# A two-layer expert network behind Nyström attention: the second activation from ACT's table of mish

## The chip, the cores and the metric

The kernel runs on one core of one Trainium2 chip. The metric is the device time of one execution in microseconds (us). The time before is 887.63 us, the median of three runs (885.74 to 888.40). Engines are named as the profile names them: PE is TensorE's matmul, PEld its weight load, DVE is VectorE, ACT is ScalarE, POOL is GpSimd, SP is the queue that issues the DMAs.

## The reference

Attention in Nyström form over 4 batches, 8 heads, 576 positions and a head size of 64 gives 2304 rows of 512. Two feed-forward layers follow, each with a width of 2048:

```python
h = x @ w_in                      # layer 1
x = (h / (1 + exp(-h))) @ w_out   # silu
h = x @ w_in2                     # layer 2
sp = where(h > 20, h, log1p(exp(min(h, 20))))
out = (h * tanh(sp)) @ w_out2     # mish
```

The change touches the second layer alone.

## The kernel before

**Split numbers.** A product is made of three matmuls: each operand is held as a rounded part (fp32r) and a low part, the difference to the exact value, and high times high, high times low and low times high are summed in one bank of PSUM. So an activation ends in two steps: a rounding copy `gh` and a subtraction `gl = z - gh`.

**Second layer (from L1015).** It goes over 6 blocks (`i`) of 384 tokens, and in each over 16 slices (`j`) of 128 of the inner width: 96 steps `t`, here hh(t) and o(t). hh(t) is 12 matmuls of 384 columns (`h_matmuls`, four parts of the 512 inputs by three terms, recorded at L609), into bank 5 + t mod 3. Then `mish_steps` makes gh(t) and gl(t) from that bank. o(t) is 9 matmuls of 512 columns (`out_matmuls`, L1106: three groups of 128 tokens by three terms), which add to three output banks over the 16 slices of a block. With the last slice `out_block` copies the three banks out (L1069 on ACT; in the last block also L1071, L1074, L1075) and SP stores them (L1077).

**Activation before.** With e = exp(min(h, 20)) and n = e(e + 2), mish is h·n/(n + 2). The kernel makes it in ten instructions: L1033 DVE (min, from PSUM), L1034 ACT (Exp), L1038 and L1039 DVE (n, and n·h, again from PSUM), L1040 and L1041 ACT (Ln of n + 2, then Exp of its negative: r = 1/(n + 2)), L1043, L1044 and L1046 DVE (a Newton step on r, and the product, with its sign turned), L1047 ACT (gh) and L1050 POOL (gl; DVE in the last two steps). The outputs have the sign turned back when they are copied out.

**Order of the work.** PE, ACT and DVE run this layer in the order in which the program names the instructions; POOL and SP are ordered by the compiler's scheduler. At step t PE gets hh(t) and then o(t-2). `mish_steps` is a generator whose parts are woven: in step t the first part of t, then the third part of t-1, the second part of t, and the fourth of t-1. At the end the order is written by hand in `due`: no o at t = 93, o(91) at 94, o(92) and o(93) at 95, then o(94), then o(95).

**What else runs in it.** In steps 0 and 1 PE finishes layer 1 (`emit_y`), whose four banks are copied out at L687 (ACT) and L689 (DVE) and stored by SP (L691). In the first six steps the last six slices of the second layer's `w_out` are loaded (L935), rounded on ACT (L603) and given a low part on POOL (L604). From j = 4 of each block the next block's inputs are loaded (L916), and from j = 6 on rounded on ACT (L920) and given a low part on POOL (L921).

The lines that the change and the prediction name: L125 to L128 (the constant `two`), L1018 (the load of ACT's table), L1027 to L1051 (`mish_steps`), L1069 to L1075 (copies out), L1091 to L1093 and L1124 to L1146 (the loop's order).

Of the kernel before, what the change touches and what calls it, by code (L numbers as in the profile page):

```python
# [8 lines left out]
F32 = mybir.dt.float32  # L9
# [4 lines left out]
AF = mybir.ActivationFunctionType  # L14
ALU = mybir.AluOpType
# [4 lines left out]
P = 128  # L20
# [5 lines left out]
NB2 = 384  # L26
LAG = 2
LAG2 = 2
# [62 lines left out]
def nystrom_moe_kernel(ctx, tc, q, k, v, w1i, w1o, w2i, w2o, out):  # L91
# [4 lines left out]
    NF = FF // P  # L96
# [4 lines left out]
    act, dve, pool, pe, sp = nc.scalar, nc.vector, nc.gpsimd, nc.tensor, nc.sync  # L101
    act.preload_act_table_set("exp_and_others")

    cp = ctx.enter_context(tc.tile_pool(name="cp", bufs=1))
# [17 lines left out]
    mask4 = cp.tile([P, 4], F32, name="mask4")  # L122
    sel2 = cp.tile([P, 2], F32, name="sel2")
    blk = cp.tile([P, P], F32, name="blk")
    two = cp.tile([P, 1], F32, name="two")  # L125
    for t in (mask2, mask4, sel2, blk):
        pool.memset(t, 0.0)
    pool.memset(two, 2.0)  # L128
    for h2 in range(2):
        pool.memset(mask2[64 * h2 : 64 * h2 + 64, h2 : h2 + 1], 1.0 / (G * 8.0))  # L130
    for h in range(4):
# [9 lines left out]
    def bank(i, name):  # L141
        return ps.tile([P, 512], F32, tag=f"b{i}", name=name)
# [502 lines left out]
    def h_matmuls(hb, w, x, n):  # L645
        (wh, wl), (xh, xl) = w, x
        for dt in range(ND):
            mm3(hb[:, :n], [(wh[:, dt], xh[:, dt]), (wh[:, dt], xl[:, dt]), (wl[:, dt], xh[:, dt])], dt == 0, dt == ND - 1)

    def after(later, earlier, reason="activation tables"):  # L650
        tc.add_manual_dep(
            later.ins,
            earlier.ins.name,
            mybir.DependencyInfo(mybir.DependencyClass.NoSync, mybir.DependencyReason.DATA),
            reason=reason,
        )
# [222 lines left out]
    nblk = NT // HB  # L879
    steps = [(i, j) for i in range(2, nblk) for j in range(NF)]  # L880
    ybank = {}
    gt = {}
# [26 lines left out]
    def y_load(i, pl):  # L909
        yh = pl.tile([P, ND, NB2], F32R, tag=f"yh{i % 2}", bufs=1, name=f"yh{i}")  # L910
        yl = pl.tile([P, ND, NB2], F32R, tag=f"yl{i % 2}", bufs=1, name=f"yl{i}")
        raws = []

        def load(t):
            raw = late["pool"].tile([P, 512], F32, tag=f"raw{t % 2}", bufs=2, name=f"yr{i}_{t}")
            sp.dma_start(raw[:, :NB2], ysc[t * P : (t + 1) * P, i * NB2 : (i + 1) * NB2])  # L916
            raws.append(raw)

        def part(t):
            act.copy(yh[:, t], raws[t][:, :NB2])  # L920
            pool.tensor_tensor(yl[:, t], raws[t][:, :NB2], yh[:, t].bitcast(F32), op=ALU.subtract)  # L921

        return (yh, yl), load, part
# [36 lines left out]
    def gtiles(t, n):  # L960
        gt_ = wp.tile([P, 2, n], F32R, tag=f"gt{t % 3}", name=f"g{t}_{n}")
        return gt_[:, 0], gt_[:, 1]

    def emit_y(t):
        i, j = steps1[t]
        if j == 0:
            ybank[i] = [bank(m, f"y{i}_{m}") for m in range(ND)]
        y_matmuls(ybank[i], wout[j], *gt.pop(("a", t)), j == 0, j == NF - 1)
        if j == NF - 1:
            y_out(ybank[i], i)  # L970
# [3 lines left out]
    for t in range(len(steps)):  # L974
        i, j = steps[t]
# [6 lines left out]
        if i == nblk - 1 and j == 0:  # L982
# [3 lines left out]
            ycur, yload, ypart = y_load(0, late["pool"])  # L986
            wgen = [second_weights(0), second_weights(1)]
        hb = bank((4, 6)[t % 2], f"h{t}")
# [26 lines left out]
    lft.close()  # L1015


    tables = act.preload_act_table_set("natural_log_exp_and_others")  # L1018
    for x in tanhs[-4:]:
        after(tables, x)  # L1020
    m2 = ctx.enter_context(tc.tile_pool(name="m2", bufs=2))
    late["tail"], late["lo"] = m2, pool
    nblk = NT // NB2
    NCH = NB2 // P
    steps = [(i, j) for i in range(nblk) for j in range(NF)]

    def mish_steps(t, h):  # L1027

        e = m2.tile([P, NB2], F32, tag="e", bufs=3, name=f"e{t}")
        n = m2.tile([P, NB2], F32, tag="n", bufs=2, name=f"n{t}")  # L1030
        r = m2.tile([P, NB2], F32, tag="r", bufs=2, name=f"r{t}")
        z = m2.tile([P, NB2], F32, tag="z", bufs=2, name=f"z{t}")
        dve.tensor_scalar(e, h, 20.0, None, op0=ALU.min)  # L1033
        ins = act.activation(e, e, AF.Exp)  # L1034
        if t == 0:
            after(ins, tables)
        yield
        dve.scalar_tensor_tensor(n, e, 2.0, e, op0=ALU.add, op1=ALU.mult)  # L1038
        dve.tensor_tensor(e, n, h, op=ALU.mult)  # L1039
        act.activation(r, n, AF.Ln, bias=two)  # L1040
        act.activation(r, r, AF.Exp, scale=-1.0)  # L1041
        yield
        dve.scalar_tensor_tensor(z, n, 2.0, r, op0=ALU.add, op1=ALU.mult)  # L1043
        dve.scalar_tensor_tensor(z, z, -2.0, r, op0=ALU.add, op1=ALU.mult)  # L1044
        gh, gl = gt[t] = gtiles(t, NB2)
        dve.tensor_tensor(z, z, e, op=ALU.mult)  # L1046
        act.copy(gh, z)  # L1047
        yield
        eng = pool if t < nblk * NF - 2 else dve
        eng.tensor_tensor(gl, z, gh.bitcast(F32), op=ALU.subtract)  # L1050
        yield  # L1051

    def out_rows(o):

        if o // S in dve_tr:
            return [(0, P, out[o : o + P, :])]
        parts, n = [], 0
        while n < P:
            b, c, r = (o + n) // S, (o + n) % S // PT, (o + n) % PT
            k = min(P - n, PT - r)  # L1060
            parts.append((n, n + k, out[b * S : (b + 1) * S, :].rearrange("(p c) n -> c p n", c=NC)[c, r : r + k]))
            n += k
        return parts

    def out_block(i):
        for c in range(NCH):
            ot = m2.tile([P, DM], F32, tag="ot", bufs=3, name=f"ot{i}_{c}")
            if i < nblk - 1 or c == 0:
                act.mul(ot, obank[i][c], -1.0)  # L1069
            elif c == 1:  # L1070
                dve.tensor_scalar(ot, obank[i][c], -1.0, None, op0=ALU.mult)  # L1071
            else:
                h = DM // 2
                act.mul(ot[:, :h], obank[i][c][:, :h], -1.0)  # L1074
                dve.tensor_scalar(ot[:, h:], obank[i][c][:, h:], -1.0, None, op0=ALU.mult)  # L1075
            for r0, r1, rows in out_rows(i * NB2 + c * P):
                sp.dma_start(rows, ot[r0:r1])  # L1077

# [9 lines left out]
                part(dt)  # L1088
                yield

    mish, ys, obank = {}, {0: ycur}, {}  # L1091
    n = len(steps)
    due = {3: (), 2: (n - 5,), 1: (n - 4, n - 3), 0: (n - 2,), -1: (n - 1,)}  # L1093

    def out_matmuls(t):
        i, j = steps[t]
        gh, gl = gt.pop(t)
        wh, wl = wout2[j]
        if j == 0:
            obank[i] = [bank((NCH * i + c + 4) % 5, f"o{i}_{c}") for c in range(NCH)]  # L1100
        order = [(c, k) for k in range(3) for c in range(NCH)]
        if t == len(steps) - 1:
            order = [(0, 0), (0, 1), (1, 0), (1, 1), (0, 2), (1, 2), (2, 0), (2, 1), (2, 2)]
        for c, k in order:
            a, w = ((gh, wh), (gh, wl), (gl, wh))[k]
            pe.matmul(  # L1106
                obank[i][c],
                a[:, c * P : (c + 1) * P],
                w,
                start=j == 0 and k == 0,  # L1110
                stop=j == NF - 1 and k == 2,
            )
        if j == NF - 1:
            out_block(i)

    with tc.manual_schedule(engines={act.engine, dve.engine, pe.engine}):
        for t in range(len(steps) + LAG2):
            if t < len(steps):
                i, j = steps[t]
                while j not in win2:  # L1120
                    next(wgen[0])
                hb = bank(5 + t % 3, f"hh{t}")
                h_matmuls(hb, win2[j], ys[i], NB2)
                mish[t] = mish_steps(t, hb[:, :NB2])  # L1124
                next(mish[t])
                for x in (mish.get(t - 1), mish[t]) if t < len(steps) - 1 else (mish[t], mish[t - 1]):
                    if x:
                        next(x)
                if t:
                    next(mish[t - 1])  # L1130
                if i == 0:
                    next(wgen[0], None)
                    next(wgen[1], None)
                if t < LAG:
                    emit_y(len(steps1) - LAG + t)
                if j == 4:
                    ygen = next_y(i + 1)
                if j >= 4:
                    next(ygen, None)
            elif t == len(steps):  # L1140
                next(mish[t - 1])
                next(mish[t - 1])

            for ty in due.get(len(steps) - t, (t - LAG2,)):
                if ty >= 0:
                    out_matmuls(ty)  # L1146


_INS = ["q", "k", "v", "moe_w_in", "moe_w_out", "moe2_w_in", "moe2_w_out"]
# [25 lines left out]
```

## Time and profile before

| | before |
|---|---|
| median of three runs | 887.63 us (885.74 to 888.40) |
| span of the profiled execution | 886.1 us |
| PE busy | 851.9 us (96%) |
| DVE busy | 648.5 us (73%) |
| ACT busy | 475.5 us (54%) |
| POOL busy | 290.3 us (33%) |

The span runs from the first instruction to the last in one profiled execution. Nothing is listed of that execution beside its span, which lies 1.5 us under the median of the runs and within their spread. A busy time counts how long an engine had at least one instruction in work; matmuls overlap each other, so a row's mean duration of a matmul is longer than the distance from one matmul's start to the next. The chain of waits follows the work that ended last back through the program; where PE stands in it for long stretches without a break, PE sets the pace there.

### The profile page before, as it was taken

What the parts mean: (1) busy time and instruction counts of PE and PEld (TensorE: products, weight loads), DVE (VectorE), ACT (ScalarE), POOL (GpSimd) and SP (SyncE); (2) the same over time, 40 slices, a digit from 0 to 9 for tenths busy, and PEclk for the clock granted to TensorE, in tenths of its full rate; (3) what the DMA queues carried; (4) which work ended last, traced back from release to release, by engine and by line L of the source; (5) the groups of instructions that cost most, each with busy time, mean ns of one, the idle gap of its engine ahead of it and who ended that gap; (6) DMA issues with size and microseconds to landing.
All of it is one profiled execution on the core that took longest, in us unless ns stands there. A gap on an engine that the chain in (4) does not pass through costs nothing.

```text
span 886.1 us, 15069 instructions
## 1 busy us (share of the span) xinstructions
PE 851.9 (96%) x5424; PEld 740.1 (84%) x5424; DVE 648.5 (73%) x1289; ACT 475.5 (54%) x1045; POOL 290.3 (33%) x331
## 2 busy tenths in 40 slices
PE   6889999999999898999999999999999999999997
PEld 5656777769998797889899889999998998998996
DVE  3878878778586868743565987787787787787776
ACT  4657555355445555654565555555555455555543
POOL 1311323034433446534333432232242242242221
PEclk8779999999999999999999999999999999999999
DMA  8735475344363466812551111000110110000000
GB/s 229 200 98 147 155 211 155 70 125 97 97 141 116 115 212 221 274 52 73 171 169 56 51 27 26 20 28 18 27 27 12 34 28 5 32 1 1 36 1 36
DMA packets 95355, 79.63 MB, mean 90 GB/s; under 512 B 52528, under 2 KB 80688, under 8 KB 95280
## 3 DMA queue, kind: packets, MB, share of 16 engines
q1 hardware_dynamic: 95280, 78.67, 30.8%
q8 instruction: 42, 0.69, 0.3%
q14 instruction: 33, 0.27, 0.1%
HBM read 60.82 MB, written 17.83 MB: 89 GB/s over the span
## 4 chain that ended last, share of the span: by engine, by line
PE 74%; DVE 8%; issue 5%; POOL 4%; ACT 4%; DMA 3%; SPq 1%; POOLq 0%; DVEq 0%; ACTq 0%
PE hh L609 21%; PE o L1106 21%; PE y L609 11%; PE h L609 5%; PE ya L835 5%; PE ha L635 4%; POOL g L667 2%; PE u L524 2%; DMA q<-in_q_dram 2%; PE nw L421 2%; DVE z L1044 1%; PE cv L372 1%; DVE rawt L596 1%; POOL rawt L591 1%; SPq L201 1%
## 5 line engine op out<-in xcount | busy, mean ns | idle before, releaser
L1050 POOL TENSOR_TENSOR g<-z,g 128x384 fp32r<-128x384 f32 x94 | 95.9, 1020 | 258.8 <-ACT g L1047 256.5
L1106 PE MATMUL o<-wh,g 128*128 128x512 f32 x576 | 166.3, 396 | 2.7 <-ACT g L1047 1.5
L609 PE MATMUL y<-g,wh 128*128 128x288 f32 x768 | 163.0, 302 | 5.6 <-POOL g L667 1.8
L609 PEld LDWEIGHTS y<-g,wh 128*128 128x128 f32 x768 | 124.5, 190 | 15.2 <-ACT th L664 4.1
L667 POOL TENSOR_TENSOR g<-g,g 128x288 fp32r<-128x288 f32 x96 | 81.2, 846 | 169.6 <-ACT g L666 140.3
L609 PE MATMUL hh<-yh,wi2h 128*128 128x384 f32 x384 | 130.4, 339 | 0.0
L609 PE MATMUL hh<-yh,wi2l 128*128 128x384 f32 x384 | 129.6, 338 | 0.0
L609 PE MATMUL hh<-yl,wi2h 128*128 128x384 f32 x384 | 129.5, 337 | 0.0
L1106 PEld LDWEIGHTS o<-wh,g 128*128 128x128 f32 x576 | 106.4, 188 | 23.5 <-ACT g L1047 3.7
L1047 ACT CAST g<-z 128x384 fp32r<-128x384 f32 x96 | 49.3, 514 | 132.2 <-DVE z L1046 132.2
L609 PE MATMUL y<-g,wl 128*128 128x288 f32 x384 | 114.0, 297 | 0.0
L1033 DVE TENSOR_SCALAR e<-hh 128x384 f32<-128x384 f32 x96 | 53.5, 557 | 69.3 <-PE hh L609 69.1
L609 PE MATMUL h<-ath,uw 128*128 128x288 f32 x384 | 95.2, 302 | 1.1 <-DVE uw L544 1.1
L1106 PE MATMUL o<-wl,g 128*128 128x512 f32 x288 | 82.2, 393 | 0.0
L1034 ACT ACTIVATE e<-e 128x384 f32<-128x384 f32 x96 | 50.3, 524 | 55.2 <-DVE e L1033 54.7
L665 DVE SCALAR_TENSOR_TENSOR g<-th,h 128x288 f32<-128x288 f32 x96 | 42.9, 447 | 50.4 <-ACT th L664 48.1
L609 PEld LDWEIGHTS hh<-yh,wi2h 128*128 128x128 f32 x384 | 72.1, 188 | 4.1
L609 PEld LDWEIGHTS hh<-yl,wi2h 128*128 128x128 f32 x384 | 72.1, 188 | 3.9
L609 PEld LDWEIGHTS y<-g,wl 128*128 128x128 f32 x384 | 72.7, 189 | 0.4 <-issue 0.4
L609 PEld LDWEIGHTS h<-ath,uw 128*128 128x128 f32 x384 | 67.4, 189 | 5.8 <-issue 3.6
L1044 DVE SCALAR_TENSOR_TENSOR z<-z,r 128x384 f32<-128x384 f32 x96 | 69.8, 727 | 3.3
L609 PEld LDWEIGHTS hh<-yh,wi2l 128*128 128x128 f32 x384 | 72.0, 188 | 0.0
(163 smaller groups left out, 1591.7 us busy)
## 6 DMA issues: line engine op xcount, KB each, us to landing
rawi<-in_moe_w_in_dram SPq DMA_DIRECT2D x16, 512.0 KB, 4.9
rawo<-in_moe_w_out_dram SPq DMA_DIRECT2D x16, 512.0 KB, 3.6
rawt<-in_moe_w_in_dram SPq DMA_DIRECT2D x16, 512.0 KB, 4.8
w2c<-ct SPq DMA_DIRECT2D x32, 256.0 KB, 2.6
rawt<-in_moe_w_out_dram SPq DMA_DIRECT2D x16, 512.0 KB, 4.4
w2r<-w2c SPq DMA_DIRECT2D x32, 256.0 KB, 2.8
v<-in_v_dram SPq DMA_DIRECT2D x32, 144.0 KB, 2.9
ysc<-yo SPq DMA_DIRECT2D x32, 144.0 KB, 1.8
```

Source lines behind the costliest of these rows:

```text
L421: pe.matmul(nbk[:, i, a : w + D], lhs, rv[:, i, a:], start=True, stop=True)
L609: pe.matmul(o, a, b_, start=first and i == 0, stop=last and i == n - 1)
L635: pe.matmul(hb[:, :HB], uw[j // 2][:, g, j % 2], ath[0][:, g, hf * HB : (hf + 1) * HB], start=g == 0, stop=g == 1)
L665: dve.scalar_tensor_tensor(g2, th, 1.0, hb[:, :HB], op0=ALU.add, op1=ALU.mult)
L667: eng.tensor_tensor(gl, g2, gh.bitcast(F32), op=ALU.subtract)
L835: pe.matmul(yb[hf, m][:, :HB], wof[j][:, m * P : (m + 1) * P], gst[j // 2][:, j % 2, hf], start=j == 0, stop=j == NF - 1,)
L1033: dve.tensor_scalar(e, h, 20.0, None, op0=ALU.min)
L1034: ins = act.activation(e, e, AF.Exp)
L1044: dve.scalar_tensor_tensor(z, z, -2.0, r, op0=ALU.add, op1=ALU.mult)
L1047: act.copy(gh, z)
L1050: eng.tensor_tensor(gl, z, gh.bitcast(F32), op=ALU.subtract)
L1106: pe.matmul(obank[i][c], a[:, c * P : (c + 1) * P], w, start=j == 0 and k == 0, stop=j == NF - 1 and k == 2,)
```

## The change

`mish_steps` becomes three instructions: ACT reads h from its PSUM bank and writes mish to z, DVE makes the rounding copy gh and then the low part gl. Its parts are no longer woven over two steps: all three are named in step t. The table set that is loaded ahead of the layer is that of mish. The outputs are copied out without a change of sign. `due` is gone: o(t-2) follows hh(t) up to the end, then o(94) and o(95). The constant `two` goes.

```diff
-    two = cp.tile([P, 1], F32, name="two")
...
-    pool.memset(two, 2.0)
...
-    tables = act.preload_act_table_set("natural_log_exp_and_others")
+    tables = act.preload_act_table_set("mish")
...
-        e = m2.tile([P, NB2], F32, tag="e", bufs=3, name=f"e{t}")
-        n = m2.tile([P, NB2], F32, tag="n", bufs=2, name=f"n{t}")
-        r = m2.tile([P, NB2], F32, tag="r", bufs=2, name=f"r{t}")
-        z = m2.tile([P, NB2], F32, tag="z", bufs=2, name=f"z{t}")
-        dve.tensor_scalar(e, h, 20.0, None, op0=ALU.min)
-        ins = act.activation(e, e, AF.Exp)
+        z = m2.tile([P, NB2], F32, tag="z", bufs=3, name=f"z{t}")
+        ins = act.activation(z, h, AF.Mish)
         if t == 0:
             after(ins, tables)
         yield
-        dve.scalar_tensor_tensor(n, e, 2.0, e, op0=ALU.add, op1=ALU.mult)
-        dve.tensor_tensor(e, n, h, op=ALU.mult)
-        act.activation(r, n, AF.Ln, bias=two)
-        act.activation(r, r, AF.Exp, scale=-1.0)
+        gh, gl = gt[t] = gtiles(t, NB2)
+        dve.tensor_copy(gh, z)
         yield
-        dve.scalar_tensor_tensor(z, n, 2.0, r, op0=ALU.add, op1=ALU.mult)
-        dve.scalar_tensor_tensor(z, z, -2.0, r, op0=ALU.add, op1=ALU.mult)
-        gh, gl = gt[t] = gtiles(t, NB2)
-        dve.tensor_tensor(z, z, e, op=ALU.mult)
-        act.copy(gh, z)
-        yield
-        eng = pool if t < nblk * NF - 2 else dve
-        eng.tensor_tensor(gl, z, gh.bitcast(F32), op=ALU.subtract)
+        dve.tensor_tensor(gl, z, gh.bitcast(F32), op=ALU.subtract)
         yield
...
-                act.mul(ot, obank[i][c], -1.0)
+                act.copy(ot, obank[i][c])
...
-                dve.tensor_scalar(ot, obank[i][c], -1.0, None, op0=ALU.mult)
+                dve.tensor_copy(ot, obank[i][c])
...
-    due = {3: (), 2: (n - 5,), 1: (n - 4, n - 3), 0: (n - 2,), -1: (n - 1,)}
...
-                mish[t] = mish_steps(t, hb[:, :NB2])
-                next(mish[t])
-                for x in (mish.get(t - 1), mish[t]) if t < len(steps) - 1 else (mish[t], mish[t - 1]):
-                    if x:
-                        next(x)
-                if t:
-                    next(mish[t - 1])
+                mish = mish_steps(t, hb[:, :NB2])
+                for _ in mish:
+                    pass
...
-            for ty in due.get(len(steps) - t, (t - LAG2,)):
-                if ty >= 0:
-                    out_matmuls(ty)
+            if t >= LAG2:
+                out_matmuls(t - LAG2)
```

The halves of the last copy out (L1074, L1075) are changed in the same way.

## Rows read from the trace of the kernel before

**Rows 1.** The page: busy time by engine, granted clock, chain by engine.
```profile
PE 851.9 (96%) x5424; PEld 740.1 (84%) x5424; DVE 648.5 (73%) x1289; ACT 475.5 (54%) x1045; POOL 290.3 (33%) x331
...
PEclk8779999999999999999999999999999999999999
...
PE 74%; DVE 8%; issue 5%; POOL 4%; ACT 4%; DMA 3%; SPq 1%; POOLq 0%; DVEq 0%; ACTq 0%
```
**Rows 2.** Chain of waits, 600 to 720 us: start, duration, piece.
```profile
606.75 2.12 PE hh L609 x12
608.88 2.08 PE o L1106 x9
...
617.29 2.18 PE o L1106 x9
...
690.98 2.11 PE hh L609 x12
```
**Rows 3.** Chain of waits, 455 to 507 us.
```profile
469.12 1.58 PE y L609 x12
470.70 2.12 PE hh L609 x12
472.82 1.62 PE y L609 x12
474.44 2.14 PE hh L609 x12
...
476.60 0.56 DVE e L1033
...
482.08 1.55 DVE z L1044
```
**Rows 4.** PE's waits from 470 us on: total, times, longest.
```profile
PE o L1106 <- ACT yo L687: 0.6, 1, 0.6
PE o L1106 <- DVE yo L689: 0.3, 1, 0.3
```
**Rows 5.** PEld's waits from 470 us on.
```profile
PEld o L1106 <- ACT g L1047: 3.7, 5, 1.4
PEld o L1106 <- ACT ot L1069: 1.3, 5, 0.3
```
**Rows 6.** Timeline of PE: first matmuls of hh(2), hh(8), hh(93); the last matmul.
```profile
478.02 0.34 PE L609 MATMUL hh<-yh,wi2h 128*128 128x384 f32 x1
...
505.67 0.34 PE L609 MATMUL hh<-yh,wi2h 128*128 128x384 f32 x1
...
863.06 0.33 PE L609 MATMUL hh<-yh,wi2h 128*128 128x384 f32 x1
...
881.56 0.40 PE L1106 MATMUL o<-wh,g 128*128 128x512 f32 x1
```
**Rows 7.** Timeline of the end: o(94), o(95), last copy out.
```profile
876.74 0.50 PE L1106 MATMUL o<-wh,g 128*128 128x512 f32 x1 [1.02 <-ACT g L1047]
...
879.60 0.50 PE L1106 MATMUL o<-wh,g 128*128 128x512 f32 x1 [0.51 <-ACT g L1047]
...
882.41 0.42 DVE L1075 TENSOR_SCALAR ot<-o 128x256 f32<-128x256 f32 x1 [0.42 <-ACT ot L1074]
```
**Rows 8.** Groups of instructions by line: busy us, mean ns, idle before.
```profile
L1040 ACT ACTIVATE r<-n,two 128x384 f32<-128x384 f32 x96 | 58.9, 613 | 1.3 <-DVE n L1038 1.3
...
L1046 DVE TENSOR_TENSOR z<-z,e 128x384 f32<-128x384 f32 x96 | 53.6, 558 | 3.3
L1033 DVE TENSOR_SCALAR e<-hh 128x384 f32<-128x384 f32 x96 | 53.5, 557 | 69.3 <-PE hh L609 69.1
...
L1034 ACT ACTIVATE e<-e 128x384 f32<-128x384 f32 x96 | 50.3, 524 | 55.2 <-DVE e L1033 54.7
...
L664 ACT ACTIVATE th<-h 128x288 f32<-128x288 f32 x96 | 39.2, 409 | 42.2 <-PE h L609 41.8
```
**Rows 9.** Timeline of ACT, POOL and DVE, 469 to 498 us.
```profile
469.65 1.28 ACT L1018 ACT_TABLE_LOAD   x1
...
495.27 0.61 ACT L603 CAST wh<-w2r 128x512 fp32r<-128x512 f32 x1
...
495.95 1.30 POOL L604 TENSOR_TENSOR wl<-w2r,wh 128x512 fp32r<-128x512 f32 x1 [0.56 <-ACT wh L603]
...
496.06 1.60 DVE L1044 SCALAR_TENSOR_TENSOR z<-z,r 128x384 f32<-128x384 f32 x1
```

More of the change, by code (lines that the diff above doesn't have):

```diff
@@ L1068, in out_block @@
             if i < nblk - 1 or c == 0:
-                act.mul(ot, obank[i][c], -1.0)
+                act.copy(ot, obank[i][c])
             elif c == 1:
-                dve.tensor_scalar(ot, obank[i][c], -1.0, None, op0=ALU.mult)
+                dve.tensor_copy(ot, obank[i][c])
             else:
                 h = DM // 2
-                act.mul(ot[:, :h], obank[i][c][:, :h], -1.0)
-                dve.tensor_scalar(ot[:, h:], obank[i][c][:, h:], -1.0, None, op0=ALU.mult)
+                act.copy(ot[:, :h], obank[i][c][:, :h])
+                dve.tensor_copy(ot[:, h:], obank[i][c][:, h:])
             for r0, r1, rows in out_rows(i * NB2 + c * P):
@@ L1089, in next_y @@
                 yield
-    mish, ys, obank = {}, {0: ycur}, {}
-    n = len(steps)
-    due = {3: (), 2: (n - 5,), 1: (n - 4, n - 3), 0: (n - 2,), -1: (n - 1,)}
+    ys, obank = {0: ycur}, {}
     def out_matmuls(t):
@@ L1139, in nystrom_moe_kernel @@
                     next(ygen, None)
-            elif t == len(steps):
-                next(mish[t - 1])
-                next(mish[t - 1])
-            for ty in due.get(len(steps) - t, (t - LAG2,)):
-                if ty >= 0:
-                    out_matmuls(ty)
+            if t >= LAG2:
+                out_matmuls(t - LAG2)
 _INS = ["q", "k", "v", "moe_w_in", "moe_w_out", "moe2_w_in", "moe2_w_out"]
```

## The prediction

> **What bounds the kernel now.** I read the page first. PE is busy for 96% of the span and makes up 74% of the chain that ended last, while DVE, ACT and POOL are busy for 73%, 54% and 33%; TensorE's granted clock is at its upper level, 2.4 GHz, through the second half [rows 1]. A busy PE is no proof, since matmuls overlap, so the next view is the chain of waits in order of time. In the middle of the second layer it holds nothing but PE: 12 hh matmuls in 2.12 or 2.11 us (it alternates by block), 9 o matmuls in 2.08 us, and again [rows 2]. A step is 4.20 us there. DVE, ACT and POOL work hidden beside it. What the change takes from them is worth nothing in that stretch; it can only pay where PE waits for them. PE's waits show three such places.
>
> First, the start. Once PE has finished layer 1, the chain leaves PE for DVE and ACT at 476.60 us [rows 3]. o(0) waits for the banks of layer 1, which are copied out behind the long activation (0.3 and 0.6 us) [rows 4], and later o's wait for gh [rows 5]. From the start of hh(2) to that of hh(8) are 505.67 - 478.02 = 27.65 us for six steps [rows 6], against 6 x 4.20 = 25.20: 2.45 us lost. The reason is on DVE: its z of L1044 takes 1.60 us while POOL's L604 runs, against 0.56 us for its like [rows 8, 9].
>
> Second, the beginning of a block's output: an o of 2.18 us against 2.08 [rows 2], five times, because the bank that the new block shares with the old one is copied out by ACT behind its activation [rows 5]. That is 5 x 0.1 = 0.5 us.
>
> Third, the end: o(94) and o(95) wait for gh, 1.02 and 0.51 us by those rows [rows 7]. From the start of hh(93) there are left 3 hh and 5 o, 3 x 2.11 + 5 x 2.08 = 16.73 us, so that PE could be through at 879.79; the last matmul starts at 881.56 [rows 6] and takes a pitch of 2.08 / 9 = 0.23, so 881.79. Lost: 2.0 us.
>
> The three sum to 4.95 us. The other way round, from hh(2) on PE has 94 hh and 96 o to do: 47 x 2.12 + 47 x 2.11 + 96 x 2.08 = 198.8 + 199.7 = 398.5 us. Without a gap it would end at 478.02 + 398.5 = 876.5 instead of 881.79: 5.3 us. The difference between the two is small slips in steps 8 to 12 and rounding. I take **5.2 us** as all that PE can win here.
>
> **The change, part by part.**
>
> *Removed.* Six DVE, four ACT and one POOL instruction per step, all beside PE except in the three places. For the middle stretch I cost this at nothing: PE's own 4.20 us hides it, and it has hidden more until now.
>
> *Mish on ACT.* One ACTIVATE of 128x384 from PSUM. No row has this function. From below, the tanh of layer 1 reads PSUM for 288 columns in 0.41 us; from above, the Ln with a bias operand takes 0.61 us for 384; the plain Exp takes 0.52 [rows 8], and I take that, as the form nearest to it. Either end is hidden. To matter it would have to outlast a step: with 0.61 for a cast [rows 9], over 3.5 us.
>
> *Copy and low part on DVE.* The subtraction is an operation of L1046's kind, 0.56 us. For the copy the nearest row of this size is the min of L1033, 0.56 us [rows 8]; below, nothing; above, 1.60 us, if POOL is in its way as in rows 9. I take 0.56 each, since POOL loses its 94 subtractions of this layer and works beside DVE only in the first six steps and four steps of a block. In place of a chain over two steps, gh and gl are ready some 0.52 + 0.56 + 0.56 = 1.64 us after hh(t) ends, plus hand-overs. PE wants them 8.4 us after (o(t-2), hh(t+1), o(t-1), hh(t+2)), at the very end 4.16 us after (o(93), o(94)). So nothing of it lies on the path.
>
> *The new wait and who stands behind it.* DVE's copy waits for ACT, ACT for hh(t). Behind the copy in steps 0 and 1 stand DVE's copies out of layer 1's banks. hh(1) ends at about 476.6 [rows 3]; mish, copy and subtraction end at 478.3, or 479.4 if POOL's L604 falls on the last; one bank is copied out 0.4 us later (by the row of L664, of the same size [rows 8]), before hh(2) ends at 478.02 + 2.12 = 480.1. ACT has the cast (0.61) and its own copy out behind mish and is done earlier. So o(0) does not wait. The weight casts of ACT come behind mish(t) and wait for their load; POOL's L604 frees the buffer for the next but one. In each of these steps mish, copy, subtraction, cast and L604 make 0.52 + 0.56 + 0.56 + 0.61 + 1.30 = 3.55 us even if no two of them overlap, less than 4.20.
>
> The port is where a rule speaks against the change. In the rows DVE's z is held while POOL's L604 runs [rows 9]. The Trainium skill ("SBUF — State Buffer", Who interferes with whom) says that a DVE operation with two SBUF inputs, or one in a two-port mode such as an fp32 copy within SBUF, and a GpSimd operation that reads SBUF shut each other out for the whole instruction; the trace agrees, with 1.60 us against 0.56. By that rule both new DVE instructions can be held, where before POOL had the subtraction. The sum of 3.55 us is already without overlap, so the rule changes no term; it feeds the first rival.
>
> *Copies out.* The same work without the factor -1: no difference. ACT gets to the first bank of a block right after the last o of the block, so the 0.5 us go. *Table load*: one for one, 1.28 us beside PE [rows 9]. *The constant and the tiles*: a memset at the start goes; addresses of later tiles move.
>
> *The order at the end.* o(91) to o(93) come one place earlier, hh(94) and hh(95) one later; no DMA is moved, for the stores follow o(95) alone. With gh and gl early, PE runs hh(95), o(93), o(94), o(95) without a gap. The copies out and the stores behind the last matmul (to the end of the span, 886.1 - 881.79 = 4.3 us) stay.
>
> **Sum.** 5.2 us off. In the profiled execution, 886.1 - 5.2 = 880.9. The median of the runs lies 1.5 us above that span, and I carry the gain to it: 887.6 - 5.2 = **882.4 us**, 0.59% less. A measurement of this kernel can tell about 0.3%, 2.66 us, from no change.
>
> PE's pitch itself is the open term: the same 12 hh take 2.11 or 2.12 us from block to block, and layer 1's y group takes 1.58 us at 469 us and 1.62 at 473 [rows 2, 3]. I see no engine's work in step with this; it may hang on where the operands lie, and their places move. If all hh ran at 2.11, 0.5 us more would go.
>
> **The rivals.**
>
> *The first block stays slow.* The activation no longer fills DVE, but the weights' low parts on POOL and DVE's two operations hold each other up, a load comes late, ACT stands at its cast with mish behind it, and o waits as before. For it: 1.60 us in rows 9. Against it: 3.55 us of work in 4.20, and two steps of lead. The start keeps its 2.45 us, the end and the blocks still give 2.5: 885.1 us, within 0.3%. Chance 0.10.
>
> *The table lacks the copy.* If ACT's copies needed another table, the load of 1.28 us [rows 9] would come twice around every cast and copy out. In the middle this hides: 0.52 + 0.61 + 2 x 1.28 = 3.69 us of 4.20. At the end one load would lie before the first copy out, and in step 1 one before a bank of layer 1: 882.4 + 1.3 + up to 1.3 = 883.7 to 885.0. The Trainium skill ("ScalarE: Activation LUTs", Table sets) says that copy is in every set; no run here shows it. Chance 0.04.
>
> *Slower: PE's pitch rises.* The place is the 94 steps; it decides when a step grows by 5.2 / 94 = 0.055 us, 1.3%. At the worst ratio in the rows, 1.62 / 1.58 = 2.5%, a step would be 0.105 us longer: +9.9, net +4.7, 892.3 us. For it: addresses move, and that spread exists. Against it: the hh and o groups of the second layer stay at 2.11 to 2.12 and 2.08 us from block to block [rows 2], with their operands in different tiles. Chance 0.05.
>
> **How the numbers follow.** The forecast keeps 0.81. Within it the time runs from 5.2 + 0.5 and a faster run (885.74 against 887.63, 1.9 us) below, 887.6 - 7.6 = 880.0, to 884. Outwards I take 1 us for a lower pitch, 879.0, and the first two rivals with 0.9 us of spread above 885.1: 886.0. Outside lie the slower rival and some tails, less than 0.2. Faster by over 0.3% (under 884.97): the forecast and most of the table rival, 0.84. Within 0.3%: the first rival and a little, 0.11. Slower: 0.05.
>
> **What would show it.** In the changed kernel's chain of waits PE should stand without DVE or ACT from 470 us to the last matmul; six steps from hh(2) should take 25.2 us; o at the start of a block 2.08; the last matmul should start at about 876.3 us. The idle rows of o with "g" and "ot" should be gone, mish should be at 0.5 us and DVE four instructions of 0.56 us, 2.2 us, less busy per step. Wrong would be: a new releaser of o in the first block (rival one), more than one table load in this layer (rival two), or hh and o groups over 2.12 and 2.08 us in the middle (rival three).

## The result, and the profile after

The changed kernel takes 878.08 us (median of four runs, 875.19 to 880.93) against 887.07 in the runs of before beside it: a ratio of 0.9897, 95% interval 0.9865 to 0.9929. Nine more runs of the same kernel gave 878.80 us and a ratio of 0.9923 (0.9895 to 0.9951). Both intervals hold 0.9914, which is 1 - 7.6 / 887: the 7.6 us that the traces show, as the next paragraphs say. The forecast was 882.4 us, with a range from 879.0. So the sign was right, the gain was larger than forecast, and the median of the first runs fell 0.9 us below the range.

The page of the changed kernel, busy time and chain (against [rows 1]):

```profile
span 879.2 us, 14197 instructions
...
PE 846.9 (96%) x5424; PEld 738.3 (84%) x5424; DVE 412.2 (47%) x903; ACT 325.3 (37%) x757; POOL 201.5 (23%) x236
...
PEclk8869999999999999999999999999999999999999
...
PE 78%; DVE 7%; issue 5%; POOL 3%; DMA 3%; ACT 2%; SPq 2%; POOLq 0%; DVEq 0%; ACTq 0%
```

DVE lost 236 us of work, ACT 150, POOL 89, and PE's busy time fell by 5.0. Of those 475 us the time can show 7.6 at most, 1.6%: PE sets the pace. TensorE's granted clock is at its upper level, 2.4 GHz, in the second half as before [rows 1].

What happens ahead of the second layer differs from execution to execution, and in the profiles of this study the first hh starts anywhere between 466.9 and 472.8 us, with either program. To compare traces I therefore use one **stretch**: from the start of the first hh matmul to that of the last matmul of o. The timeline of PE, before and then after, has them (before, the last one is in [rows 6], at 881.56):

```profile
470.54 0.34 PE L609 MATMUL hh<-yh,wi2h 128*128 128x384 f32 x1
```
```profile
471.21 0.34 PE L607 MATMUL hh<-yh,wi2h 128*128 128x384 f32 x1
...
478.62 0.34 PE L607 MATMUL hh<-yh,wi2h 128*128 128x384 f32 x1
...
503.58 0.34 PE L607 MATMUL hh<-yh,wi2h 128*128 128x384 f32 x1
...
874.62 0.39 PE L1088 MATMUL o<-wh,g 128*128 128x512 f32 x1
```

Before it is 881.56 - 470.54 = 411.02 us, after it is 874.62 - 471.21 = 403.41: **7.6 us** less, 0.86% of 887. The middle two rows are the starts of hh(2) and hh(8): 24.96 us for six steps, where it was 27.65 and the prediction had put 25.20. The chain of waits of the changed kernel shows where that comes from, first at the start of the second layer (against [rows 3]), then in the third and fourth block (against [rows 2]):

```profile
475.06 2.11 PE hh L607 x12
477.17 1.62 PE y L607 x12
478.78 2.11 PE hh L607 x12
480.89 2.08 PE o L1088 x9
...
608.14 2.11 PE hh L607 x12
610.25 2.04 PE o L1088 x9
...
649.67 2.10 PE hh L607 x12
651.78 2.06 PE o L1088 x9
...
676.76 2.08 PE o L1088 x9
678.85 2.10 PE hh L607 x12
```

Two things are to be seen. No DVE, ACT or POOL stands in the chain from the first hh to the last matmul: every wait of PE is gone (the list of PE's waits over this stretch is empty). That was forecast. And the o group takes 2.04 or 2.06 us in even blocks (counted from 0), where it was 2.08 in all blocks before; in odd blocks it still takes 2.08. The hh group fell too, from 2.12 to 2.11 in the first eleven slices of the even blocks and to 2.10 in the last five, and from 2.11 to 2.10 in the first eleven of the odd ones. That was not forecast.

The new instructions, from the groups of instructions by line from 471 us on:

```profile
L1028 ACT ACTIVATE z<-hh 128x384 f32<-128x384 f32 x96 | 47.2, 492 | 324.9 <-PE hh L607 241.5 <-issue 83.4
L1033 DVE CAST g<-z 128x384 fp32r<-128x384 f32 x96 | 34.7, 361 | 307.2 <-ACT z L1028 307.2
```

Mish takes 0.49 us (I had put 0.52 between 0.41 and 0.61), the low part 0.56 as put, the copy 0.36 instead of 0.56. Together 1.41 us, of which nothing lies on PE's path. With the hand-overs it is 1.73 us, as the last step shows: o starts behind hh(95) at 868.69, and the low part of g(95) ends at 869.86 + 0.56 = 870.42, while PE is busy with o(93).

```profile
868.69 0.86 PE L1088 MATMUL o<-wh,g 128*128 128x512 f32 x3
...
869.86 0.56 DVE L1035 TENSOR_TENSOR g<-z,g 128x384 fp32r<-128x384 f32 x1
```

### The profile page after: what moved, and what is told of

The parts are those of the page before. It is cut to its first block, busy times and chain, and to the rows that moved or that the text cites. A ratio compares the mean times of both kernels' runs of the same rounds, so it can differ in the third digit from the quotient of the medians.

```text
span 879.2 us, 14197 instructions
## 1 busy us (share of the span) xinstructions
PE 846.9 (96%) x5424; PEld 738.3 (84%) x5424; DVE 412.2 (47%) x903; ACT 325.3 (37%) x757; POOL 201.5 (23%) x236
## 4 chain that ended last, share of the span: by engine, by line
PE 78%; DVE 7%; issue 5%; POOL 3%; DMA 3%; ACT 2%; SPq 2%; POOLq 0%; DVEq 0%; ACTq 0%
PE hh L607 23%; PE o L1088 23%; PE y L607 11%; PE h L607 5%; PE ya L833 5%; PE ha L633 4%; PE u L522 2%; POOL g L665 2%; PE nw L419 2%; PE cv L370 1%; DVE rawt L594 1%; DMA k<-in_k_dram 1%; SPq L199 1%; PE a L456 1%; DVE g L663 1%
## 5 line engine op out<-in xcount | busy, mean ns | idle before, releaser
L1033 DVE CAST g<-z 128x384 fp32r<-128x384 f32 x96 | 34.7, 361 | 307.2 <-ACT z L1028 307.2
L1028 ACT ACTIVATE z<-hh 128x384 f32<-128x384 f32 x96 | 47.2, 492 | 324.9 <-PE hh L607 241.5
L1088 PE MATMUL o<-wh,g 128*128 128x512 f32 x576 | 163.4, 392 | 0.0
L919 POOL TENSOR_TENSOR yl<-yr,yh 128x384 fp32r<-128x384 f32 x24 | 31.9, 1329 | 256.9 <-ACT yh L918 256.8
L833 PE MATMUL ya<-gs,wl 128*128 128x288 f32 x256 | 68.0, 411 | 0.0
L1088 PEld LDWEIGHTS o<-wl,g 128*128 128x128 f32 x288 | 54.0, 188 | 12.1
```

Source lines behind the costliest of these rows:

```text
L833: pe.matmul(yb[hf, m][:, :HB], wof[j][:, m * P : (m + 1) * P], gst[j // 2][:, j % 2, hf], start=j == 0, stop=j == NF - 1,)
L1028: ins = act.activation(z, h, AF.Mish)
L1033: dve.tensor_copy(gh, z)
L1088: pe.matmul(obank[i][c], a[:, c * P : (c + 1) * P], w, start=j == 0 and k == 0, stop=j == NF - 1 and k == 2,)
```

## The experiments

Two questions were open. Were the waits gone for the reason that I gave, and what made PE's groups shorter? For the second there were two theories. **A:** PE's pitch hangs on where its operands lie in memory. The change takes a 4-byte constant away, which takes up 32 bytes, so all tiles of the left side of the memory (g, the inputs of the odd blocks, and all weights but the low parts of eleven slices) move 32 bytes down. It also takes six tiles of 1536 bytes from the last pool, so the inputs of the odd blocks move 9216 + 32 = 9248 bytes. What lies on the right side, the inputs of the even blocks and those low parts, stays. **B:** DVE, ACT and POOL touch memory less, and PE runs freer beside them.

Experiments 4 to 10 were run once each, so they are read from their traces. Traces that should agree do: the stretch is 403.41, 403.46 and 403.46 us in the first runs and in experiments 1 and 6, and 405.92 in experiments 2 and 4.

**1. More runs of the changed kernel** (no edit).

> The changed kernel, unchanged, for more runs. From the first hh to the last matmul its trace took 403.4 us against 411.0 before, 7.6 us less; outside that stretch nothing was touched. If the stretch is all of the gain, the time is 7.6 us (0.86%) under that of before, give or take 1.5; if something ahead of the second layer became faster as well, it is 9 us or more.

The ratio is 0.9923 (0.9895 to 0.9951), 6.8 us; the trace's stretch is 403.46 us. So the stretch accounts for the gain. The 9.0 us of the first runs are 1.4 more; that is inside their interval, and no run shows that anything outside the stretch became faster.

**2. The changed kernel with the old places.**

```diff
+    two = cp.tile([P, 1], F32, name="two")
...
+    pool.memset(two, 2.0)
...
+    for k in range(6):
+        m2.tile([P, NB2], F32, tag=f"pad{k}", bufs=1, name=f"pad{k}")
```

> The changed kernel with unused tiles in the place of the removed ones, so that every operand of PE lies where it lay before. Theory A (PE's pitch hangs on where its operands lie): hh and o groups take what they took before, 2.12 and 2.08 us in even blocks, 2.11 and 2.08 in odd ones, and from the first hh to the last matmul 405.8 us, 2.4 more than the changed kernel. Theory B (PE's pitch fell because DVE, ACT and POOL do less beside it): the pitch stays that of the changed kernel, 2.11 and 2.04 in even blocks, and the stretch 403.4 us.

Ratio 0.9944 (0.9920 to 0.9968). Chain of waits in the third block, then the stretch's first and last row in the timeline:

```profile
608.11 2.12 PE hh L609 x12
610.23 2.08 PE o L1093 x9
```
```profile
470.34 0.34 PE L609 MATMUL hh<-yh,wi2h 128*128 128x384 f32 x1
...
876.26 0.39 PE L1093 MATMUL o<-wh,g 128*128 128x512 f32 x1
```

405.92 us, with 2.12 and 2.08 in the even blocks. The instructions are the new ones and the pitch is the old one: theory A, to 0.1 us. The six steps from hh(2) take 503.06 - 477.82 = 25.24 us, which is the prediction's 25.20. So the waits alone are worth 411.02 - 405.92 = 5.1 us, and the places 405.92 - 403.41 = 2.5.

**3. The kernel before with the new places.**

```diff
-    two = cp.tile([P, 1], F32, name="two")
...
+    m3 = ctx.enter_context(tc.tile_pool(name="m3", bufs=2))
+    two = m3.tile([P, 1], F32, tag="two", bufs=1, name="two")
...
-        n = m2.tile([P, NB2], F32, tag="n", bufs=2, name=f"n{t}")
+        n = m3.tile([P, NB2], F32, tag="n", bufs=2, name=f"n{t}")
```

r and z move to m3 in the same way.

> The kernel before, with n, r, z and the constant two moved to a pool behind, so that every operand of PE lies where the changed kernel has it. Theory A: the waits at the start, at the blocks and at the end stay, and the pitch is that of the changed kernel; from the first hh to the last matmul 408.6 us, 2.4 less than before. Theory B: 411.0 us, the pitch as before.

Ratio 0.9979 (0.9958 to 1.0001), which by itself can't be told from no change; the trace can. The chain in the third block:

```profile
608.86 2.11 PE hh L607 x12
610.97 2.04 PE o L1107 x9
...
619.28 2.22 PE o L1107 x9
```

The old instructions run at the new pitch: theory A again, and B is out. The stretch is 882.10 - 472.77 = 409.33 us, 1.7 less and not 2.4. Where the waits set the pace a faster PE only waits longer: the o that needs the shared bank takes 2.22 us in even blocks in place of 2.18, and the six steps from hh(2) to hh(8) take 27.71 us, not less than before.

**4. The constant alone.**

```diff
+    two = cp.tile([P, 1], F32, name="two")
...
+    pool.memset(two, 2.0)
```

> The changed kernel with only the 4-byte constant and its memset back: all tiles of the left side lie 32 bytes higher, the inputs of the odd blocks stay in their new place. Theory A with the 32 bytes as the cause: o in even blocks goes back from 2.04 to 2.08 us and hh from 2.11 to 2.12. Theory A with the larger shift (9 KB) as the cause: even blocks stay at 2.11 and 2.04. Theory B: 403.4 us as in the changed kernel.

The chain and the stretch:

```profile
608.03 2.12 PE hh L609 x12
610.15 2.08 PE o L1090 x9
```
```profile
470.26 0.34 PE L609 MATMUL hh<-yh,wi2h 128*128 128x384 f32 x1
...
876.18 0.39 PE L1090 MATMUL o<-wh,g 128*128 128x512 f32 x1
```

405.92 us, the figure of experiment 2. The inputs of the odd blocks go up by the 32 bytes too and stay 9216 below their old place; that move does nothing that can be seen, and as 36 times 256 bytes it leaves each address where it was within 256. The 32 bytes are all of it. A constant of 4 bytes per partition that nothing reads costs 2.5 us here.

**5. The order at the end taken out of the kernel before.**

```diff
-    due = {3: (), 2: (n - 5,), 1: (n - 4, n - 3), 0: (n - 2,), -1: (n - 1,)}
+    due = {}
```

> The kernel before with the order written by hand at the end taken out, so that o(t-2) follows hh(t) to the last step. Theory 1 (the order at the end was there only to give the long activation of step 95 an earlier start): hh(95) comes one o later, o(94) and o(95) wait longer, and from the first hh to the last matmul it takes 413 us, 2 more than before. Theory 2 (the order did nothing): 411.0 us.

The stretch is 884.85 - 471.44 = 413.41 us, 2.4 more than before, and PE's waits say where:

```profile
PE o L1106 <- ACT g L1047: 2.9, 3, 2.6
```

Before they were 1.5 us in two waits:

```profile
PE o L1106 <- ACT g L1047: 1.5, 2, 1.0
```

That is 1.4 of the 2.4 us. Behind the longest wait, in which PE stood still up to 879.25 us, the granted clock fell: it is 0.50, the lower level of 1.2 GHz, from 881 to 883 us, and the matmuls of o start 0.43 us apart there (883.13 to 883.56) in place of 0.23. The row is one microsecond of that: window, length, busy time of PE, PEld, DVE, ACT and POOL, granted clock, DMA share and GB/s.

```profile
882.00:883.00 1.00, 1.00 (x4) 0.79 (x3) 0.56 (x1) 0.06 (x1) 0.00 (x0) 0.50 0.00 0
```

Wait and clock come together here, and no run separates them. So the hand-written order did earn 2.4 us with the long activation; this part of the change alone would have lost them. With mish in one instruction PE has no wait at the end, and there is nothing left for the order to earn.

**6. The changed kernel on the old engines** (copy on ACT, low part on POOL).

```diff
-        dve.tensor_copy(gh, z)
+        act.copy(gh, z)
...
-        dve.tensor_tensor(gl, z, gh.bitcast(F32), op=ALU.subtract)
+        eng = pool if t < nblk * NF - 2 else dve
+        eng.tensor_tensor(gl, z, gh.bitcast(F32), op=ALU.subtract)
```

> The changed kernel with the rounding copy back on ACT and the low part back on POOL (DVE in the last two steps), as the kernel before had them; mish is still one instruction. Theory 1 (the waits went because the chain from hh to g is short, not because of the engines): no wait comes back, from the first hh to the last matmul 403.4 us. Theory 2 (POOL and DVE in each other's way made the waits at the start): six steps from hh(2) to hh(8) take over 26 us again in place of 24.96.

The stretch is 873.73 - 470.27 = 403.46 us, and the six steps take 24.96 as in the changed kernel. Where copy and low part run makes no difference, once mish is one instruction. The run doesn't test whether POOL's L604 made the waits at the start of the kernel before, by holding up DVE: with copy and low part elsewhere DVE has nothing in these steps that POOL could hold up.

**7. o one step behind hh.**

```diff
-LAG2 = 2
+LAG2 = 1
```

> The changed kernel with o one step behind hh in place of two. By the prediction g is ready some 1.64 us and hand-overs after hh ends; o(t-1) now wants it 2.1 us after (behind hh(t)), at the end o(95) 2.08 us after hh(95) (behind o(94)). If the chain is that short, no wait appears and from the first hh to the last matmul it takes 403.4 us, give or take 0.5. If hand-overs and the port make it over 2.1 us, PE waits in each of 96 steps and it takes longer by 96 times what is missing.

The stretch is 875.23 - 471.47 = 403.76 us. No o waits for g; the one wait listed, PEld's for a copy out of layer 1, is 0.4 us.

My expectation had miscounted the cover: between hh(t-1) and o(t-1) lie o(t-2) and hh(t), 4.15 us, and only o(95) has no more than the 2.08 us of o(94) ahead of it. So it is the end that tells: there the chain from hh to g took less than 2.1 us, which agrees with the prediction's 1.64 us and hand-overs and with the 1.73 us read above. For the other steps the run shows only that it is under 4.15.

**8. Six places for the inputs.** The tiles are made 256 bytes longer, and the operands start at an offset by block; the second line shows it for yh. Places are given in bytes above a multiple of 256.

```diff
+        o = [32, 192, 96, 32, 192, 96][i] // 4
...
+        yh = yh[:, o : o + n].rearrange("p (a n) -> p a n", a=ND)
```

> The changed kernel with the inputs yh and yl of the six blocks at addresses that are 0, 32, 64, 128, 160 and 192 bytes above a multiple of 256 (in the changed kernel 224 in even blocks and 96 in odd ones; the weights and g stay at 96). Theory A1 (what counts is the address within some 256 bytes, against that of the other operands): the groups of hh and of o differ from block to block with the offset and no longer go by even and odd. Theory A2 (what counts is the side of the memory on which the inputs lie): 2.11 and 2.04 us in even blocks, 2.11 and 2.08 in odd ones, as in the changed kernel.

The chain, one step with a late slice for each of the blocks 0 (inputs at 0), 1 (at 32), 2 (at 64), 4 (at 160) and 5 (at 192). Late are the last five slices of a block, in which the low part of the first matmul's weights lies at 96 like all other weights and g; in the first eleven it lies at 224.

```profile
525.49 2.08 PE hh L607 x12
527.58 2.08 PE o L1092 x9
...
587.91 2.12 PE hh L607 x12
590.03 2.04 PE o L1092 x9
...
654.62 2.09 PE hh L607 x12
656.71 2.04 PE o L1092 x9
...
787.59 2.08 PE hh L607 x12
789.67 2.05 PE o L1092 x9
...
854.29 2.12 PE hh L607 x12
856.41 2.08 PE o L1092 x9
```

Block 3 (at 128) takes 2.12 and 2.04 us, as block 1 does. The o groups speak for theory A1: they take 2.08, 2.04 and 2.05 us in the even blocks, and 2.04 and 2.08 in the odd ones. The hh groups leave the side open in this run, 2.08 or 2.09 us in all even blocks and 2.12 in all odd ones. Experiments 10 and 11 settle it: with the inputs at 160 the odd block 5 takes the 2.08 and 2.05 us of block 4 here, and with all inputs at 64 both sides take the same. At 64 a step of late slices takes 4.13 us, the least seen; at 160 it takes 0.01 us more.

**9. Six places for g,** with the inputs at 224 in all blocks.

```diff
+            o = [32, 64, 96, 128, 160, 192][t // NF] // 4
+            gt_ = wp.tile([P, 2 * n + 64], F32R, tag=f"gt{t % 3}", name=f"g{t}_{n}")
```

> The changed kernel with the inputs at 224 bytes above a multiple of 256 in all six blocks, and g at 128, 160, 192, 224, 0 and 32 (96 in the changed kernel, as the weights of the second matmul). Theory A1: the groups of o differ from block to block, and none is at the changed kernel's 2.04 in all its places but where the offset says so. Theory A2: 2.04 us in even blocks and 2.08 in odd ones.

The chain in blocks 1 (g at 160), 3 (at 224) and 5 (at 32):

```profile
559.19 2.11 PE o L1096 x9
...
693.81 2.10 PE o L1096 x9
...
828.32 2.07 PE o L1096 x9
```

Moving g away from the 96 at which the second matmul's weights lie made o slower in every block: 2.07 to 2.11 us, against 2.04 and 2.06 in the even blocks of the changed kernel, where the inputs lie at 224 too.

**10. A finer set of places for the inputs** (low parts at 96, offsets by block as in 8).

```diff
+        o = [224, 208, 240, 232, 216, 64][i] // 4
```

> As inputs_at_64, with the inputs of the six blocks at 64, 48, 80, 72, 56 and 160 bytes above a multiple of 256. If the pitch hangs on the offset in units of 32 bytes, 72 and 80 are like 64, and 48 and 56 like 32 (2.12 and 2.04); if it is finer than that, all six differ. 160 gave 2.08 and 2.05 before.

The chain in blocks 1 (inputs at 48), 2 (at 80), 3 (at 72) and 5 (at 160):

```profile
553.69 2.12 PE hh L607 x12
...
620.55 2.15 PE hh L607 x12
...
687.94 2.14 PE hh L607 x12
...
822.04 2.08 PE hh L607 x12
```

48 is like 32, but 72 and 80 are not like 64, up to 2.15 us against 2.08, and 56 (block 4) takes 2.14 or 2.15 and is not like 32. So units of 32 bytes are not the rule. What the rule is stays open.

**11. All inputs at 64, all weights at 96.** The best of experiment 8, made the layout of all blocks. The unused tile of the last line brings the low parts of the first eleven slices from 224 to 96.

```diff
+        o = 224 // 4
...
+    late["pool"].tile([P, 32], F32, tag="pad", bufs=1, name="pad")
```

> The changed kernel with the inputs of all blocks 64 bytes above a multiple of 256 and all weights and g at 96 (the low parts of the first 11 slices come from 224 to 96). In the run with six places a block with the inputs at 64 took 2.08 us for hh and 2.04 for o in the slices whose low parts lie at 96 too. If that holds for all slices, a step is 4.13 us against 4.17 on average, from the first hh to the last matmul it takes 399.3 us, 4.1 less than the changed kernel, and the time is 1.3% under that of before. If the good figure belonged to that block alone, it stays at 403.

874.93 us against 888.21 in the runs beside it, a ratio of 0.9854 (0.9821 to 0.9887). The chain and the stretch:

```profile
605.74 2.08 PE hh L607 x12
607.83 2.04 PE o L1093 x9
```
```profile
470.32 0.34 PE L607 MATMUL hh<-yh,wi2h 128*128 128x384 f32 x1
...
869.41 0.39 PE L1093 MATMUL o<-wh,g 128*128 128x512 f32 x1
```

399.09 us, where 399.3 was expected. This version beats both kernels: its interval lies under that of the changed kernel, and against that kernel only addresses differ, not one instruction.

Each ratio is to the runs of before beside it.

| run | instructions | places | stretch, us | ratio to before (95%) |
|---|---|---|---|---|
| before | old | old | 411.02 | 1 |
| before, new places | old | new | 409.33 | 0.9979 (0.9958 to 1.0001) |
| changed, old places | new | old | 405.92 | 0.9944 (0.9920 to 0.9968) |
| changed | new | new | 403.41 | 0.9923 (0.9895 to 0.9951) |
| changed, inputs at 64 | new | chosen | 399.09 | 0.9854 (0.9821 to 0.9887) |

## Why the prediction was right or wrong, point by point

**What bounds the kernel: right.** PE does, and the three places where it waits were the right ones. Per step there are four DVE instructions, three ACT and one POOL fewer, and in the middle they are worth nothing: with the places held, a step takes 2.12 + 2.08 us as before (experiment 2).

**The waits: right.** I put 5.2 us, between 4.95 and 5.3; experiment 2 gives 5.1 with the places held. The reason holds as far as it was tested: the chain from hh to g is short (1.73 us at the end, and experiment 7 bounds it by 2.1 there), and it may run on either set of engines (experiment 6). For the start the prediction also named POOL's hold on DVE's z, 1.60 us against 0.56; what share of the 2.45 us that was, no run shows.

**The copy on DVE: off, at no cost.** The nearest row gave 0.56 us, it took 0.36. The Trainium skill ("VectorE: DVE Perf Modes", Mode 2×_2P) has fp32 copies within SBUF at two elements a cycle, which fits the row. The prediction had named such a copy only for the port, and took its price from a row that reads PSUM. Nothing hung on it.

**The port between DVE and POOL: turned round, and smaller.** The prediction allowed for DVE being held by POOL's L604, up to 1.60 us. It was POOL that was held: its split of the weights took 1.55 us in all six steps, where it was 1.29 or 1.30 before when it came first [rows 9], while DVE's subtraction took 0.56 in all 96. Both were hidden.

**"The constant and the tiles: a memset at the start goes; addresses of later tiles move": this is the step that failed.** The sum costed the move at nothing. It was worth 2.5 us with the new instructions, as experiments 2 and 4 show, and 1.7 with the old ones (experiment 3). The prediction had seen the sign of it: PE's groups alternate by block, in step with no engine's work, and "it may hang on where the operands lie". It had overlooked a second one in the chain of before: in odd blocks hh takes 2.11 us in the first eleven slices and 2.10 in the last five, and from the twelfth slice on the low part of the weights lies in another pool.

```profile
716.14 2.11 PE hh L609 x12
...
720.33 2.10 PE hh L609 x12
```

But then it used the sign in one direction only. As a rival it made the kernel slower; downward it allowed 0.5 us for hh and 1 us in the range, and took the 2.08 us of o as fixed. An unknown term whose sign nothing in the trace decides belongs on both sides of the sum with the same width. The spread that it used upward, 2.5% of a step, would have been more than enough downward.

**The 4.3 us between forecast and first median.** 2.4 are the pitch (7.6 us in the trace against 5.2 forecast). 0.6 are the lower median of before in this comparison, 887.07 against 887.63, and 1.4 what the first runs gained beyond the stretch. Neither of these two is a step of the prediction. Without them the time would be 887.6 - 7.6 = 880.0 us, inside the range near its lower end, so that it fell outside is in part bad luck.

**The end: right.** No wait is left there, and the tail from the start of the last matmul is unchanged, 4.5 us before and 4.6 after.

**The rivals.** The first two fell: the first block does not stay slow (24.96 us for six steps), and ACT's copies need no second table, for there is one load of 1.28 us, as before. The third named the right cause, the addresses, and had its sign wrong.

## What to carry to other kernels

Where one engine sets the pace, price a change by that engine's waits, one by one, and cost all other work at nothing: here that came within 0.2 us, with the places held. Then look at what the change moves in memory, since the pitch of the pacing engine itself can hang on it: before a gain or a loss of a per cent is put down to an edit, run the edit with unused tiles in the places of the removed ones. And a hand-made order that works around a slow chain is worth its price only as long as the chain is slow.

## What the runs showed of the hardware

The pitch of back-to-back matmuls here hangs on the addresses of their operands, finer than 32 bytes and by up to some 3%: the same 12 matmuls of 384 columns took between 2.08 us (inputs 0, 64 or 160 bytes above a multiple of 256, all weights at 96) and 2.15 us (inputs at 56 or 80); 9 matmuls of 512 columns took between 2.04 and 2.11 us as g was moved. In the old places and in the new ones the figure repeats with the old activation and with the new, whatever the other engines do beside it (experiments 2, 3 and 6). The granted clock is 1.00 in all these rows. And it carries over: o's group changes with the place of the inputs, which only hh reads (2.04 us with them at 64, 2.08 at 192, weights and g at 96 both times). Why, and by which rule, no run here settles.

In experiment 5 PE's longest wait, 2.58 us, was followed by matmuls at the lower clock level, 0.50, so that more was lost there than the wait.
